# The first four feed-forward quanta of a fused attention and feed-forward kernel, laid side by side in four PSUM banks around AV of the fourth head pair

## The chip, the core and the metric

The kernel runs on one core of a Trainium2 chip. The metric is the device time of one execution in microseconds (us), as the median of several runs. One further execution was recorded by the hardware profiler; all durations and waits below come from it. The engines are named as in the profile: PE is TensorE (matmuls; PEld its weight loads), DVE is VectorE, ACT is ScalarE, POOL is GpSimd and SP is SyncE, which here only issues DMAs.

## What is computed

Attention with a relative-position bias, and then a bilinear feed-forward layer on its output:

```python
B, H, S, D = 8, 8, 576, 64
scores = (1 / sqrt(D)) * matmul(q, k.transpose(0, 1, 3, 2))
scores = scores + bias_table[bucket].transpose(2, 0, 1)[None]
attn = exp(scores - max(scores)); attn = attn / (sum(attn) + 1e-09)
attn_out = matmul(attn, v)
x = attn_out.transpose(0, 2, 1, 3).reshape(B * S, H * D)      # 4608 x 512
return (x @ w_a) * (x @ w_b) @ w_out                           # 512 -> 1536 -> 512
```

## The kernel before

The work of attention is cut into 32 head pairs (batch b, pair hp of heads 2hp and 2hp+1), numbered p = 4b + hp. For each pair: q and k are brought into the layout "channels on partitions" (`emit_transposes_first` and `emit_transposes` on PE for p below 10, a transposing DMA after that), scores are computed transposed (`emit_scores`, four tiles st_0 to st_3 of 128 keys by 2 x 512 queries; `emit_scores_rest`, st_4 and st_5 for what is left over), ACT takes their exponential into a tile `at`, DVE multiplies in the exponential of the bias where it isn't constant (`emit_mult`), and PE multiplies with v (`emit_av`, ten groups per pair, called AV here). A column of ones beside v gives the sums; DVE divides by them (L331, L333) into a tile `xg`. `emit_x` transposes `xg` into `xn`, the transposed x that the feed-forward needs: on PE with a copy by DVE for the first batch, by a transposing DMA for the others. Head pair hp of a batch gives the 128 rows `xn[:, hp, ...]`, so the sum over the 512 model channels has four parts, mc = 0 to 3, and part mc needs only head pair mc.

The feed-forward works on nine chunks c of 512 tokens. It is written as a generator, `ffn_quanta`, of 36 quanta a chunk, each of four matmuls of 512 columns: for each of 12 blocks df of the hidden channels a quantum "pa" (x times w_a, four parts mc, into one PSUM bank; ACT copies the bank to a tile `ha`) and a quantum "pb" (x times w_b; DVE multiplies the bank by `ha` into `g`), and then 12 quanta "po" (`g` times w_out, three quanta to one output tile, which DVE copies and SP sends out). Quanta are pulled one by one with `next(quanta)` and so fill PE between the steps of attention.

The order on each engine is written by hand (a manual schedule): every engine works through its instructions in the order of emission, and semaphores only delay them. PSUM has eight banks of 2 KB a partition. Four of them are a ring of two slots with two banks each (`pst`, tag "st"), for the scores and the transposes of q and k. The other four are single banks, m0 to m3, given out in turn by `bank(use, ...)`: at first m0 and m1 to the use "av" (AV results, transposes of x), m2 and m3 to "ffn".

The first four pairs (batch 0) run in the loop at L442. The feed-forward can't start before all four pairs have their rows in `xn`: L475 to L485 emit x of pair 2, AV of pair 3, x of pair 3, and only then the first two quanta (pa 0, pb 0), the transposes of pair 4's q and k, and two more quanta (pa 1, pb 1). From there "av" has the bank m0 alone and "ffn" has m1, m2 and m3. `QUANTA_FIRST` says how many quanta of the first chunk are done by then (4). The main loop at L498 has nine places s for each pair from p = 4 on; at each place it emits scores (s = 0, 3, 6), multiplications (s = 2, 5, 8), perhaps a quantum (L522: the remaining 36 - QUANTA_FIRST quanta of the first chunk are spread over the first 47 places, from then on each place has one), and parts of AV of the pair before (`AV_AT`, `AV_LAST`). In pair 5 at s = 3, `relayout_qk(1, 4, 8)` (L525) lets DVE copy q and k of pairs 6 and 7 into the layout that their transposes (`emit_transposes`, L219) read; it stands behind the quantum of its place. The loads of v, of q and k and of the weights are issued by POOL in a fixed order; later loads are held back by `pace(p)`, a small copy on POOL that waits for the last multiplication of a pair.

Of the kernel before, what the change touches and what calls it, by code (L numbers as in the profile page):

```python
# [13 lines left out]
def kernel(  # L14
# [11 lines left out]
    nc = tc.nc  # L26
    FP32 = mybir.dt.float32
    BF16 = mybir.dt.bfloat16
    ACTF = mybir.ActivationFunctionType
    MULT = mybir.AluOpType.mult  # L30
# [3 lines left out]
    B, H, S, Dh = 8, 8, 576, 64  # L34
# [4 lines left out]
    NDF = DF // 128  # L39
    NMC = DM // 128  # L40
# [8 lines left out]
    wrk = ctx.enter_context(tc.tile_pool(name="wrk", bufs=2))  # L49
    pst = ctx.enter_context(tc.tile_pool(name="pst", bufs=2, space=PSUM))  # L50
# [5 lines left out]
    def bank(use, shape, dtype, name):  # L56
        turn[use] += 1
        return pone.tile(shape, dtype, tag=f"m{banks[use][turn[use] % len(banks[use])]}", name=name)
# [79 lines left out]
    wa_sb = wpool.tile([128, NMC, DF], BF16, name="wa")  # L138
    wb_sb = wpool.tile([128, NMC, DF], BF16, name="wb")
# [63 lines left out]
    xn = wpool.tile([128, NMC, NT + 64], BF16, name="xn")  # L203
# [21 lines left out]
    def emit_transposes_first(p, k_act=False, ring=False):  # L225

        b, hp = pairs[p]
        qkT = wrk.tile([128, 2, S], BF16, tag="qkT", bufs=3, name=f"qkT{p}")
        qkT_of[p], qT_of[p], kT_of[p] = qkT, qkT[:, 0, :], qkT[:, 1, :]
        both = pst.tile([128, 2, 1024], BF16, tag="st", name=f"tr{p}") if ring else None  # L230
        for which, t in enumerate(qk_tiles[b][0:2]):
            if ring:
                ps = both[:, which, :]
            else:
                ps = bank("ffn", [128, 1024], BF16, f"tr{p}_{which}")
            for j in range(LJ):
                for hh in range(2):
                    nc.tensor.transpose(ps[64 * hh:64 * hh + 64, LP * j:LP * j + LP],
                                        t[:, 2 * hp + hh, Dh * j:Dh * j + Dh], ident[0:LP, 0:LP])
            o = qkT[:, which, :].rearrange("c (p j) -> c p j", j=LJ)  # L240
            i = ps[:, 0:S].rearrange("c (j p) -> c p j", j=LJ)
            if ring:
                if which:
                    nc.scalar.activation(
                        out=qkT[:, :, :].rearrange("c w (p j) -> c w p j", j=LJ),
                        in_=both[:, :, 0:S].rearrange("c w (j p) -> c w p j", j=LJ), func=ACTF.Copy)
            elif which == 0 or k_act:
                nc.scalar.activation(out=o, in_=i, func=ACTF.Copy)
            else:
                nc.vector.tensor_copy(out=o, in_=i)  # L250

    def emit_tails(p):

        for hh in range(2):
            r = slice(64 * hh, 64 * hh + 64)
            nc.vector.tensor_copy(out=bd2[p % 2][r, :, r], in_=qkT_of[p][r, :, 512:S])
# [51 lines left out]
    def emit_av(p, gidx):  # L308

        b, hp = pairs[p]  # L310
        at, vb = at2[p % 2], vb2[b % 2]
        jq, hh = gidx // 2, gidx % 2
        if gidx in (0, 6):
            n = 3 if gidx == 0 else 2
            av_state[p] = bank("av", [128, n, 2, Dh + 1], FP32, f"av{p}_{gidx}")
        pav = av_state[p]
        j = jq if jq < 3 else jq - 3
        if hh == 0:

            nc.tensor.matmul(out=pav[:, j, :, :], lhsT=at[:, 8, 128 * jq:128 * jq + 128],  # L320
                             rhs=vb[:, 2 * hp:2 * hp + 2, 4, :], start=True, stop=False)
        for i in range(4):
            nc.tensor.matmul(out=pav[:, j, hh, :], lhsT=at[:, 2 * i + hh, 128 * jq:128 * jq + 128],  # L323
                             rhs=vb[:, 2 * hp + hh, i, :], start=False, stop=(i == 3 and hh == 1))
        if gidx in (5, 9):
            n = 3 if gidx == 5 else 2
            j0 = 0 if gidx == 5 else 3
            if gidx == 5:
                xg_of[p] = wrk.tile([128, 5, 128], BF16, tag="xg", name=f"xg{p}")
            rc = wrk.tile([128, 3, 2, 1], FP32, tag="rc", name=f"rc{p}_{gidx}")  # L330
            nc.vector.reciprocal(out=rc[:, 0:n, :, :], in_=pav[:, :, :, Dh:Dh + 1])  # L331
            xo = xg_of[p][:, j0:j0 + n, :]
            nc.vector.tensor_tensor(out=xo.rearrange("p j (h d) -> p j h d", h=2),  # L333
                                    in0=pav[:, :, :, 0:Dh],
                                    in1=rc[:, 0:n, :, :].to_broadcast([128, n, 2, Dh]), op=MULT)

    def emit_x(p):

        b, hp = pairs[p]
        if b > 0:  # L340

            nc.sync.dma_start_transpose(
                out=xn[:, hp, S * b:S * b + 640].rearrange("p (j t) -> p j t", j=5),
                in_=xg_of[p][:, :, :].rearrange("p j t -> p (j t)"))
            return
        ps = bank("av", [128, 5, 128], BF16, f"xT{p}")
        for jq in range(5):
            nc.tensor.transpose(ps[:, jq, :], xg_of[p][:, jq, :], ident[:, :])
        nc.vector.tensor_copy(out=xn[:, hp, S * b:S * b + S],  # L349
                              in_=ps[:, :, :].rearrange("p j t -> p (j t)")[:, 0:S])  # L350


    def ffn_bank(name):
        return bank("ffn", [128, 512], FP32, name)

    def ffn_quanta(c):
        g = wrk.tile([128, NDF, 512], BF16, tag="g", name=f"g{c}")
        for df in range(NDF):
            ps = ffn_bank(f"pa{c}_{df}")
            for mc in range(NMC):  # L360
                nc.tensor.matmul(out=ps[:, :], lhsT=wa_sb[:, mc, 128 * df:128 * df + 128],  # L361
                                 rhs=xn[:, mc, 512 * c:512 * c + 512],
                                 start=(mc == 0), stop=(mc == NMC - 1))
            ha = wrk.tile([128, 512], FP32, tag="ha", name=f"ha{c}_{df}")
            nc.scalar.activation(out=ha[:, :], in_=ps[:, :], func=ACTF.Copy)  # L365
            yield
            ps = ffn_bank(f"pb{c}_{df}")
            for mc in range(NMC):
                nc.tensor.matmul(out=ps[:, :], lhsT=wb_sb[:, mc, 128 * df:128 * df + 128],  # L369
                                 rhs=xn[:, mc, 512 * c:512 * c + 512],  # L370
                                 start=(mc == 0), stop=(mc == NMC - 1))
            nc.vector.tensor_tensor(out=g[:, df, :], in0=ps[:, :], in1=ha[:, :], op=MULT)  # L372
            yield
        for tt in range(4):
            ps = ffn_bank(f"po{c}_{tt}")
            for part in range(3):
                for df in range(4 * part, 4 * part + 4):
                    nc.tensor.matmul(out=ps[:, :], lhsT=g[:, df, 128 * tt:128 * tt + 128],  # L378
                                     rhs=wo_sb[:, df, :], start=(df == 0), stop=(df == NDF - 1))
                if part == 2:  # L380
                    ob = wrk.tile([128, DM], FP32, tag="ob", name=f"ob{c}_{tt}")
                    nc.vector.tensor_copy(out=ob[:, :], in_=ps[:, :])  # L382
                    r0 = 512 * c + 128 * tt
                    nc.sync.dma_start(out=out[r0:r0 + 128, :], in_=ob[:, :])
                yield

    def all_quanta():
        for c in range(NCH):
            yield from ffn_quanta(c)

    quanta = all_quanta()


    warm = const.tile([128, 512], BF16, name="warm")
# [8 lines left out]
            nc.tensor.matmul(out=wp[:, :], lhsT=warm[:, 0:128], rhs=warm[:, :], start=True, stop=True)  # L403


    QUANTA_FIRST = 4

    emit_warm(6)
    qk_alloc(0)
# [27 lines left out]
    def emit_avs(p, g0, g1):  # L437
        for g in range(g0, g1):
            emit_av(p, g)


    for p in range(4):  # L442
        emit_scores(p, 0)
        emit_scores(p, 1)
        if p:
            emit_mult(p, 0)
            emit_mult(p, 1)
            if p > 1:
                emit_x(p - 2)
                emit_avs(p - 1, 0, 4)  # L450
        else:
            emit_warm(3)
# [19 lines left out]
        emit_mult(p, 4)  # L472
        if p < 3:
            emit_tails(p + 1)
    emit_x(2)  # L475
    emit_avs(3, 0, 10)
    emit_x(3)
    banks.update(av=(0,), ffn=(2, 3, 1))
    next(quanta)
    next(quanta)  # L480
    emit_transposes_first(4, ring=True)
    emit_tails(4)
    relayout_qk(1, 2, 4)
    for _ in range(QUANTA_FIRST - 2):
        next(quanta)  # L485


# [10 lines left out]
    for p in range(4, NP + 1):  # L498
        if p < NP:
            b, hp = pairs[p]  # L500
# [5 lines left out]
        for s in range(9):  # L506
# [14 lines left out]
            n = 9 * (p - 4) + s  # L521
            if n >= 47 or (n + 1) * (36 - QUANTA_FIRST) // 47 > n * (36 - QUANTA_FIRST) // 47:  # L522
                next(quanta, None)
# [66 lines left out]
```

## Time and profile before

| | |
|---|---|
| time, median of 3 runs | 419.52 us (418.82 to 420.39) |
| the profiled execution's own time | 419.12 us |
| its span, first to last instruction | 417.4 us |
| PE busy | 402.5 us, 96% of the span |
| DVE busy | 233.9 us, 56% |
| ACT busy | 231.2 us, 55% |
| POOL busy | 79.0 us, 19% |
| granted PE clock, mean | 0.998 |

How to read the lines that follow: a line of a timeline has the start in us from the span's start, the length in us, the engine, the line in the kernel, the operation, what it writes and reads, shape and type, the number of instructions merged into it, and in brackets the idle time of the engine just before with what ended it. The end of a matmul is modelled, and matmuls overlap: one of 512 columns is shown with 379 ns, but the next starts 216 ns after it. A few matmul records are missing from the trace, so that a group of four can show three. A line of the stretches has a start and an end in us, the length, the busy time of each engine, the granted clock and the work of the DMA engines.

### The profile page before, as it was taken

How to read it: one execution, taken by the hardware profiler on the slowest of the kernel's cores; microseconds unless marked ns; L12 is line 12 of the kernel's file. 1: busy time of each engine (PE TensorE's matmuls, PEld its weight loads, DVE VectorE, ACT ScalarE, POOL GpSimd, SP SyncE). 2: the span in 40 equal slices, each digit the busy share in tenths (PEclk: the TensorE clock that was granted, in tenths of full speed). 3: DMA queues.
4: the chain of work that ended last, by engine and by line, in shares of the span. 5: the costliest groups of instructions: out<-in, count | busy, mean ns of one | idle time of the engine just before them, and what ended most of it. 6: DMA issues, size and time to landing. Idle time of an engine off the chain costs nothing.

```text
span 417.4 us, 8452 instructions
## 1 busy us (share of the span) xinstructions
PE 402.5 (96%) x3346; PEld 206.4 (49%) x3404; DVE 233.9 (56%) x568; ACT 231.2 (55%) x313; POOL 79.0 (19%) x136
## 2 busy tenths in 40 slices
PE   8789899999999999999999999999999999999996
PEld 2455355555455455454555555454554554444442
DVE  3486666676555755575556656665556553332331
ACT  4984788566755665476646674567556631321320
POOL 8744641113111311103011311130000000000000
PEclk9999999999999999999999999999999999999999
DMA  9999999699759686978697977983342012002002
GB/s 111 183 209 206 166 189 105 135 208 158 107 94 207 114 100 104 213 102 112 102 178 136 134 103 151 177 127 52 71 121 45 17 40 93 2 0 101 2 0 101
DMA packets 111176, 47.71 MB, mean 114 GB/s; under 512 B 85120, under 2 KB 106528, under 8 KB 111136
## 3 DMA queue, kind: packets, MB, share of 16 engines
q0 software_dynamic: 54304, 18.88, 42.2%
q1 hardware_dynamic: 56832, 28.29, 28.0%
q8 instruction: 26, 0.43, 0.4%
q14 instruction: 14, 0.11, 0.1%
HBM read 38.77 MB, written 16.19 MB: 132 GB/s over the span
## 4 chain that ended last, share of the span: by engine, by line
PE 85%; DMA 8%; POOL 3%; issue 2%; DVE 1%; ACT 1%; POOLq 0%; DVEq 0%
PE po L378 23%; PE pb L369 21%; PE pa L361 21%; PE av L323 8%; PE st L267 7%; DMA wb<-in_moe_w_b_dram 6%; PE av L320 2%; DMA vb<-in_v_dram 2%; PE st L285 2%; PE st L277 1%; POOL vb L129 1%; POOL kl L108 0%; PE tr L219 0%; POOL ql L108 0%; ACT at L269 0%
## 5 line engine op out<-in xcount | busy, mean ns | idle before, releaser
L269 ACT ACTIVATE at<-st 128x1024 bf16<-128x1024 f32 x128 | 124.0, 1022 | 52.1 <-PE st L267 51.2
L372 DVE TENSOR_TENSOR g<-pb,ha 128x512 bf16<-128x512 f32 x108 | 74.6, 691 | 77.0 <-PE pb L369 54.0
L365 ACT ACTIVATE ha<-pa 128x512 f32<-128x512 f32 x108 | 64.7, 599 | 92.2 <-PE pa L361 91.0
L369 PE MATMUL pb<-xn,wb 128*128 128x512 bf16 x407 | 109.0, 379 | 1.5
L361 PE MATMUL pa<-xn,wa 128*128 128x512 bf16 x417 | 108.8, 379 | 0.5
L378 PE MATMUL po<-wo,g 128*128 128x512 bf16 x415 | 99.7, 379 | 0.8
L303 DVE TENSOR_TENSOR at<-at,E 128x768 bf16<-128x768 bf16 (+2 forms) x128 | 61.5, 501 | 7.9 <-DMA E<-tab_scratch 4.1
L323 PE MATMUL av<-vb,at 128*128 128x65 bf16 x1280 | 64.7, 194 | 0.3 <-DVE at L303 0.2
L378 PEld LDWEIGHTS <-g 128*128 128x128 bf16 x432 | 39.6, 98 | 49.1 <-issue 7.9
L323 PEld LDWEIGHTS <-at 128*128 128x128 bf16 x1280 | 55.4, 98 | 16.5 <-issue 1.2
L369 PEld LDWEIGHTS <-wb 128*128 128x128 bf16 x432 | 38.7, 97 | 46.4 <-issue 8.0
L361 PEld LDWEIGHTS <-wa 128*128 128x128 bf16 x432 | 38.4, 97 | 43.2 <-issue 7.0
L382 DVE COPY ob<-po 128x512 f32<-128x512 f32 x36 | 24.9, 691 | 53.9 <-PE po L378 53.9
L267 PE MATMUL st<-qkT 64*128 64x512 bf16 x256 | 40.8, 385 | 2.6 <-ACT at L280 0.9
L320 PE MATMUL av<-vb,at 128*128 128x130 bf16 x160 | 35.4, 221 | 2.5 <-DVE xn L349 1.2
L496 POOL COPY pace<-at 1x1 bf16<-1x1 bf16 x22 | 4.2, 193 | 173.0 <-DVE at L303 172.9
L333 DVE TENSOR_TENSOR xg<-av,rc 128x384 bf16<-128x384 f32 x64 | 31.4, 491 | 2.2
L129 POOL DMA_DIRECT2D vb<-in_v_dram x36 | 30.7, 864 | 7.9 <-PE pb L369 2.2
L280 ACT ACTIVATE at<-st 128x512 bf16<-128x512 f32 x32 | 19.1, 597 | 23.0 <-PE st L277 23.0
L331 DVE RECIPROCAL rc<-av 128x6 f32<-128x6 f32 x64 | 11.8, 184 | 27.6 <-PE av L323 27.6
L320 PEld LDWEIGHTS <-at 128*128 128x128 bf16 x160 | 15.6, 98 | 17.1 <-issue 1.6
L287 ACT ACTIVATE at<-st 128x576 bf16<-128x576 f32 x32 | 20.7, 646 | 0.0
(51 smaller groups left out, 177.8 us busy)
## 6 DMA issues: line engine op xcount, KB each, us to landing
out_dram<-ob SPq DMA_DIRECT2D x36, 256.0 KB, 2.3
qk_scratch<-qkn SPq DMA_DIRECT2D x22, 288.0 KB, 4.5
ql<-in_q_dram POOLq DMA_DIRECT2D x15, 288.0 KB, 5.7
kl<-in_k_dram POOLq DMA_DIRECT2D x15, 288.0 KB, 6.9
vb<-in_v_dram POOLq DMA_DIRECT2D x28, 128.0 KB, 6.7
wa<-in_moe_w_a_dram POOLq DMA_DIRECT2D x4, 384.0 KB, 13.9
wb<-in_moe_w_b_dram POOLq DMA_DIRECT2D x4, 384.0 KB, 13.6
wo<-in_moe_w_out_dram POOLq DMA_DIRECT2D x4, 384.0 KB, 7.9
```

Source lines behind the costliest of these rows:

```text
L129: nc.gpsimd.dma_start(out=vb2[b % 2][:, h0:h1, i, 0:Dh], in_=v[b, h0:h1, 128 * i:128 * i + 128, :].transpose([1, 0, 2]))
L267: nc.tensor.matmul(out=st[:, hh, :], lhsT=kT[r, 128 * i:128 * i + 128], rhs=qT[r, 0:512], start=True, stop=True)
L269: nc.scalar.activation(out=at[:, 2 * i:2 * i + 2, 0:512], in_=st[:, :, :], func=ACTF.Exp, scale=scale)
L303: nc.vector.tensor_tensor(out=at[:, sl, q0:q0 + w], in0=at[:, sl, q0:q0 + w], in1=e, op=MULT)
L320: nc.tensor.matmul(out=pav[:, j, :, :], lhsT=at[:, 8, 128 * jq:128 * jq + 128], rhs=vb[:, 2 * hp:2 * hp + 2, 4, :], start=True, stop=False)
L323: nc.tensor.matmul(out=pav[:, j, hh, :], lhsT=at[:, 2 * i + hh, 128 * jq:128 * jq + 128], rhs=vb[:, 2 * hp + hh, i, :], start=False, stop= ...
L333: nc.vector.tensor_tensor(out=xo.rearrange("p j (h d) -> p j h d", h=2), in0=pav[:, :, :, 0:Dh], in1=rc[:, 0:n, :, :].to_broadcast([128, n ...
L361: nc.tensor.matmul(out=ps[:, :], lhsT=wa_sb[:, mc, 128 * df:128 * df + 128], rhs=xn[:, mc, 512 * c:512 * c + 512], start=(mc == 0), stop=( ...
L365: nc.scalar.activation(out=ha[:, :], in_=ps[:, :], func=ACTF.Copy)
L369: nc.tensor.matmul(out=ps[:, :], lhsT=wb_sb[:, mc, 128 * df:128 * df + 128], rhs=xn[:, mc, 512 * c:512 * c + 512], start=(mc == 0), stop=( ...
L372: nc.vector.tensor_tensor(out=g[:, df, :], in0=ps[:, :], in1=ha[:, :], op=MULT)
L378: nc.tensor.matmul(out=ps[:, :], lhsT=g[:, df, 128 * tt:128 * tt + 128], rhs=wo_sb[:, df, :], start=(df == 0), stop=(df == NDF - 1))
```

## The change

The first four quanta of the first chunk (pa 0, pb 0, pa 1, pb 1) are no longer emitted one after the other when all of x is there. They are opened together, in four PSUM banks (both banks of one slot of the score ring, and m2 and m3), and each head pair's part mc of the four sums is emitted as soon as that pair's rows of x are there: part 0 after x of pair 2 and ahead of AV of pair 3, part 1 after that AV, parts 2 and 3 after x of pair 3. The copies and products that empty the four banks follow part 3. The transposes of pair 4's q and k come after these four quanta instead of after two, and two more quanta (pa 2, pb 2) follow them, so that six are done before the main loop; the spread over its first 47 places has 30 quanta instead of 32, and the places where a quantum stands move. The copy that puts pair 2's rows into `xn` goes from DVE to ACT.

```diff
-    def emit_x(p):
+    def emit_x(p, act=False):
...
-        nc.vector.tensor_copy(out=xn[:, hp, S * b:S * b + S],
-                              in_=ps[:, :, :].rearrange("p j t -> p (j t)")[:, 0:S])
+        o, i = xn[:, hp, S * b:S * b + S], ps[:, :, :].rearrange("p j t -> p (j t)")[:, 0:S]
+        if act:
+            nc.scalar.activation(out=o, in_=i, func=ACTF.Copy)
+        else:
+            nc.vector.tensor_copy(out=o, in_=i)
...
-    def ffn_quanta(c):
-        g = wrk.tile([128, NDF, 512], BF16, tag="g", name=f"g{c}")
-        for df in range(NDF):
+    class EarlyQuanta:
+
+
+        def __init__(self):
+            self.g = wrk.tile([128, NDF, 512], BF16, tag="g", name="g0")
+            ring = pst.tile([128, 2, 512], FP32, tag="st", name="pab0_0")
+            self.ps = [(ring[:, 0, :], ring[:, 1, :]),
+                       tuple(ffn_bank(f"{n}0_1")[:, :] for n in ("pa", "pb"))]
+
+        def part(self, mc):
+            for df in range(2):
+                for ps, w_sb in zip(self.ps[df], (wa_sb, wb_sb)):
+                    nc.tensor.matmul(out=ps, lhsT=w_sb[:, mc, 128 * df:128 * df + 128],
+                                     rhs=xn[:, mc, 0:512], start=(mc == 0), stop=(mc == NMC - 1))
+                if mc == NMC - 1:
+                    ha = wrk.tile([128, 512], FP32, tag="ha", name=f"ha0_{df}")
+                    nc.scalar.activation(out=ha[:, :], in_=self.ps[df][0], func=ACTF.Copy)
+                    nc.vector.tensor_tensor(out=self.g[:, df, :], in0=self.ps[df][1], in1=ha[:, :],
+                                            op=MULT)
+
+    def ffn_quanta(c, early=None):
+        g = early.g if early else wrk.tile([128, NDF, 512], BF16, tag="g", name=f"g{c}")
+        for df in range(2 if early else 0, NDF):
...
-    def all_quanta():
+    def all_quanta(early):
         for c in range(NCH):
-            yield from ffn_quanta(c)
-
-    quanta = all_quanta()
+            yield from ffn_quanta(c, early if c == 0 else None)
...
-    QUANTA_FIRST = 4
+    QUANTA_FIRST = 6
...
-    emit_x(2)
+    emit_x(2, act=True)
+    early = EarlyQuanta()
+    early.part(0)
     emit_avs(3, 0, 10)
+    early.part(1)
     emit_x(3)
+    early.part(2)
+    early.part(3)
+    quanta = all_quanta(early)
     banks.update(av=(0,), ffn=(2, 3, 1))
-    next(quanta)
-    next(quanta)
     emit_transposes_first(4, ring=True)
     emit_tails(4)
     relayout_qk(1, 2, 4)
-    for _ in range(QUANTA_FIRST - 2):
+    for _ in range(QUANTA_FIRST - 4):
         next(quanta)
```

In the changed kernel the matmuls of the four early quanta are L371, their copies L375 and products L376; the copy of x on ACT is L351; the later quanta are L384 (pa), L388 (ha), L392 (pb), L395 (g) and L401 (po).

## The prediction

> **What bounds the kernel now.** I read the busy shares first, then the stretches of time, then the timeline of each engine where the change works.
>
> ```profile
> PE 402.5 (96%) x3346; PEld 206.4 (49%) x3404; DVE 233.9 (56%) x568; ACT 231.2 (55%) x313; POOL 79.0 (19%) x136
> ```
>
> That is each engine's busy time. Next, by stretch: its length, then busy time of PE, of weight loads, of DVE, ACT and POOL, then the granted clock.
>
> ```profile
> 32.00:50.00 18.00, 16.06 (x154) 8.05 (x156) 11.02 (x27) 11.89 (x17) 9.01 (x13) 1.00 1.47 182
> 50.00:60.00 10.00, 9.76 (x113) 5.67 (x113) 7.21 (x18) 7.49 (x11) 6.13 (x10) 1.00 1.27 201
> 60.00:70.00 10.00, 9.89 (x102) 5.47 (x101) 7.28 (x19) 8.37 (x13) 2.39 (x5) 1.00 1.66 107
> ```
>
> TensorE (PE) is the bound. In the stretch that the change touches, 32 to 50 us, it is busy 16.06 of 18.00 us; from 50 us on it has almost no holes (9.76 and 9.89 of 10). So about 1.9 us of holes is what there is to fill, and 0.24 us in the ten after that. The granted clock is 1.00 in all three. The holes, from the timeline of PE:
>
> ```profile
> 32.19 0.23 PE L320 MATMUL av<-vb,at 128*128 128x130 bf16 x1 [0.49 <-ACT at L287]
> ...
> 34.18 0.34 PE L348 MATMUL xT<-ident,xg 128*128 128x128 bf16 x3 [0.17 <-DVE xg L333]
> 34.75 0.28 PE L348 MATMUL xT<-ident,xg 128*128 128x128 bf16 x2 [0.23 <-DVE xg L333]
> ...
> 43.16 0.39 PE L267 MATMUL st<-qkT 64*128 64x512 bf16 x2 [0.57 <-ACT qkT L221]
> ...
> 49.75 0.22 PE L320 MATMUL av<-vb,at 128*128 128x130 bf16 x1 [0.67 <-DMA vb<-in_v_dram]
> ```
>
> The first is AV of the fourth pair waiting for the last exponential of its scores, the next two are the transposes of x waiting for VectorE (DVE). The fourth is a chain on ScalarE (ACT), the fifth a transfer of v that landed at 49.62 us. The last two lie behind the change; whether they give back what it gains is the question.
>
> **The change part by part.** A quantum is four 512-column matmuls; from 37.39 (pa) to 38.26 (pb) it takes 0.87 us, 0.216 a matmul. I count when PE reaches a place and how many quanta it has done by then; a quantum done early is worth 0.865 us.
>
> Step 1, the gain. Before, PE is free at about 31.6 us (end of the transposes of pair 2) and starts its second "pa" at 37.39, having done AV (five groups of two at 0.32: 1.6 us), five transposes (0.35), two quanta (1.73) and 24 transposes of q and k (0.73): 4.41 us of work in 5.79, so 1.38 us of holes. After, four quanta stand in the same stretch: 3.46 + 1.6 + 0.35 + 0.73 = 6.14 us. The first four matmuls wait only for the exponential L280, which ended at 31.59, and run until 32.5, past the end of L287 (32.14): the 0.49 is gone. The second four run while DVE divides (its last xg ends near 35.0), the third while it copies the last rows of x (near 36.0). Weights: those of rows 2 and 3 are asked for at 35.3 as before. PE is through at about 37.78, 0.39 later with 1.73 us more done: 1.34 us ahead.
>
> The copy of pair 2's x goes to ACT. No row has it; the nearest are the copy of the same shape in L248 (0.66 on ACT) and the DVE copy that it replaces (0.45). I take 0.66: it lies in a 3.86 us hole of ACT (32.14 to 36.00) and ends near 32.7, before the AV group that needs its bank (33.46). Free; without that hole it would cost up to 0.66, against 0.45 saved on DVE. The Trainium skill, "ScalarE: Activation LUTs", Rules for kernel authors, gives plain element work to VectorE, which speaks against this edit; the rows agree that ACT is the dearer (0.66 against 0.45), and an estimate by that rule would be 0.2 us worse, but the hole of 3.86 us decides.
>
> The two score banks that the first "pa" and "pb" borrow were emptied at 31.59 and are read out by 38.0; scores of pair 4 ask for them at 39.6: no wait. The two "ha" copies, 0.49 apart, end at 37.7, before the copy of q and k (L244) can start. "pb" 2 wants the bank of the second product at 38.65, when that is just read (36.95 + 0.38 for the last matmul, two DVE products of 0.69 behind the copies): no wait, or under 0.1. SP and POOL keep their order; only the pacing copies on POOL come up to a microsecond later, and the v that they pace is used some 30 us on.
>
> Step 2, the ACT chain takes one quantum back.
>
> ```profile
> 39.65 1.94 ACT L269 ACTIVATE at<-st 128x1024 bf16<-128x1024 f32 x2 [0.54 <-PE st L267]
> 41.48 0.60 ACT L365 ACTIVATE ha<-pa 128x512 f32<-128x512 f32 x1
> 41.95 1.15 ACT L221 ACTIVATE qkT<-tr 128x1152 bf16<-128x1152 bf16 x1
> 42.96 1.98 ACT L269 ACTIVATE at<-st 128x1024 bf16<-128x1024 f32 x2
> ```
>
> From the first scores of pair 4 (39.22) to its fourth score tile (43.16, which needs the bank that L221 empties) ACT works without a hole: 3.94 us, whatever PE does. Before, PE has two quanta and a transpose in that stretch; in the changed order only one quantum ("pa" 3), since the spread of 30 instead of 32 quanta over 47 places moves "pb" 3 behind the fourth tile. So PE reaches it at 43.55 with 7 quanta instead of 43.16 with 6: ahead 0.865 - 0.39 = 0.48.
>
> Step 3, it is given again at the v transfer. AV of pair 4 stood at 49.75, of which 0.78 us was idle. Now "pb" 5 and "pa" 6 come before it instead of "pa" 5, and it starts at 50.14, past the landing at 49.62, with 13 quanta done instead of 11: ahead 1.34.
>
> Step 4, a new wait on DVE.
>
> ```profile
> 51.20 0.69 DVE L372 TENSOR_TENSOR g<-pb,ha 128x512 bf16<-128x512 f32 x1 [0.73 <-remote]
> 51.80 0.71 DVE L116 COPY qkn<-ql 96x768 bf16<-96x768 bf16 x2
> 52.44 0.98 DVE L116 COPY qkn<-kl 96x768 bf16<-96x768 bf16 x2
> ```
>
> Those four copies of q and k feed the transposes of pair 6 on PE (53.05 before, no wait). In the changed order of DVE they stand behind the product of "pb" 6, and on PE "pb" 6 is followed only by one AV group and then those transposes. "pb" 6 ends issue at 52.26; its product runs 52.45 to 53.14, the first copy ends at 53.41, so the transposes, ready at 52.67, wait 0.8 us; their second half needs the third copy (54.05 to 54.2) and waits 0.35 to 0.5 more. Behind them on PE queues everything; behind the copies on DVE queues xg of pair 4, which costs the next AV group 0 to 0.2. From 50.14: four quanta 3.46, the rest 3.41, waits 1.2 to 1.4: PE starts pair 6 at 58.2 to 58.4 with 17 quanta, before at 57.64 with 16. Ahead 0.1 to 0.3.
>
> Step 5, a second one like it. In pair 6 "pb" 9 now directly precedes AV's third group, and DVE has its product ahead of the division of that group. "pb" 9 ends issue at 63.3; its product runs 63.5 to 64.2, the division ends at 64.3, xg at 64.9; the single AV bank is wanted at 64.5: a wait of 0.43. Transposes of pair 7 wait 0.13 for a score bank, about as the fourth score tile did before (0.1). Pair 7 then starts 1.03 to 1.23 later with one quantum more: 0.17 to 0.37 behind. In pair 7 two holes of before (0.18 for the AV bank, 0.12 for a score bank) shrink to one of 0.12, and by pair 8 both orders have done 28 quanta: 76.3 to 76.5 against 76.28. From there to the end the order is the same but for neighbours.
>
> Sum: 0.1 us slower, so nothing. The profiled execution took 419.12 us (span 417.4), 0.4 under the median 419.52; against it the sum gives 419.2, and against the median 419.6, which I forecast. What a measurement of this kernel can tell from no change is about 0.5%, 2.1 us.
>
> **The rivals.** The gain is kept: steps 4 and 5 do not bite, because DVE has the copies done when PE wants them. For it: DVE is busy only 7.2 of 10 us there. Against it: its order is fixed and the product needs "pb" 6. Then 1.2 to 1.4 and 0.43 us come off: 1.5 faster, 418.0.
>
> DVE's copies are slow: all four at 0.49, as the pair at 52.44 while POOL issues. The third copy then ends near 54.5, AV of the second half waits for xg, and pair 5 and pair 6 lose 0.4 to 0.8 more: 420.2.
>
> The interleaved matmuls do not keep the pitch. Before, four in a row fill one bank; L371 changes bank and weights each time, and AV cuts the sums in two. Lower end: 0.216 us, since the weight load (0.098) hides behind a matmul as in L361, and AV changes weights each time too. Upper end: the full 0.379 that one takes. 16 x 0.163 = 2.6 us: 422.2, slower; it decides by itself from a pitch of about 0.34 us. I take 0.216, because in every row of 512 columns the bank's last matmul is followed at that pitch by the next bank's first. The Trainium skill, "TensorE: Matmul & The Clock Gate", A second HAM failure mode, says that cycling through banks can leave short idle moments which make the clock fall to half; by that rule one window of 3.4 us at half rate would cost, as an estimate from that page, 1.7 us. The granted clock of 1.00 beside holes of 0.78 us speaks against it.
>
> **How the numbers follow.** No change as summed (419.0 to 420.0): 0.70. Gain kept, wholly or in part (417.8 to 419.0): 0.14. Slow copies (420.0 to 420.6): 0.10. Lost pitch: 0.04; the rest 0.02. The range runs from 418.3, most of the kept gain, to 420.6. Faster by over 0.5% needs 2.1 us, more than all the holes of 32 to 50 us: 0.03. Slower by over 0.5% is lost pitch and the unforeseen: 0.05. Within: 0.92.
>
> **What would show it.** Right: no idle before AV of the fourth pair; a longer wait for L221 at its fourth score tile of pair 4 (about 1.2 us for 0.57); no wait for v; a new wait of PE for L116 of about 0.8 us near 52.7, and one for xg near 64.5; 28 quanta done near 76.4. Wrong: the wait for L116 missing (then faster), or starts of L371 more than 0.22 us apart (then slower).

## The result, and the profile after

The changed kernel takes 421.9 us (median of 22 runs, 420.04 to 424.69), the kernel before 419.35 in the same session (22 runs, 418.24 to 422.86): a ratio of 1.0047, 95% interval 1.003 to 1.0064. So it is slower by about 2.0 us (1.3 to 2.7), not equal, and above the 420.6 at which the forecast range ended. (The two medians alone lie 2.55 us apart; the ratio with its interval, taken over the runs, is what I go by.) The profiled execution took 422.53 us, with a span of 420.8.

First the busy times, and then the same three stretches, moved by 1.68 us, since the fourth pair's last score tile (st_5 of pair 3, the last point ahead of the change) starts 1.68 us later in this profile, at 32.48 us for 30.81. The columns are as before. Ahead of the three stand two rows of the front, 10 to 32 us, of the kernel before and of the changed one.

```profile
PE 405.5 (96%) x3404; PEld 207.8 (49%) x3404; DVE 231.5 (55%) x567; ACT 231.6 (55%) x314; POOL 79.0 (19%) x136
```

```profile
10.00:32.00 22.00, 17.65 (x280) 11.38 (x281) 15.08 (x44) 20.23 (x27) 13.25 (x24) 1.00 1.30 195
...
10.00:32.00 22.00, 16.87 (x257) 11.75 (x256) 13.79 (x40) 17.56 (x24) 13.63 (x23) 0.84 1.30 192
33.70:51.70 18.00, 16.64 (x155) 8.45 (x154) 9.38 (x25) 12.26 (x18) 9.39 (x14) 1.00 1.50 193
51.70:61.70 10.00, 8.99 (x98) 4.94 (x97) 6.18 (x19) 7.29 (x11) 2.46 (x5) 1.00 1.47 192
61.70:71.70 10.00, 9.53 (x104) 5.13 (x102) 6.72 (x19) 7.91 (x11) 3.08 (x6) 1.00 0.80 67
```

The stretch of the change is fuller, as it was meant to be (PE busy 16.64 of 18.00 us for 16.06). The next two have holes that were not there: 1.0 and 0.5 us for 0.24 and 0.11. The first two rows are a stretch of the front, whose code both kernels share: its granted clock is 1.00 before and 0.84 here. The 0.84 comes from a half clock from 14.9 to 21.7 us, which the profile of before does not have; the control below shows that the change has no part in it.

The waits of PE behind the change, from its timeline:

```profile
43.73 0.39 PE L267 MATMUL st<-qkT 64*128 64x512 bf16 x2 [0.24 <-ACT at L269]
45.24 0.39 PE L267 MATMUL st<-qkT 64*128 64x512 bf16 x2 [1.12 <-ACT qkT L221]
55.28 0.97 PE L219 MATMUL tr<-ident,qkn 96*128 96x96 bf16 x12 [0.81 <-DVE qkn L116]
66.74 0.23 PE L320 MATMUL av<-vb,at 128*128 128x130 bf16 x1 [0.38 <-DVE xg L333]
...
91.17 0.38 PE L384 MATMUL pa<-xn,wa 128*128 128x512 bf16 x1 [0.56 <-DMA xn<-xg]
...
354.79 1.02 PE L384 MATMUL pa<-xn,wa 128*128 128x512 bf16 x4 [0.78 <-DVE ob L405]
```

The second, third and fourth are those that the prediction names, in the sizes that it gives; the first is a short wait for ACT ahead of the second. The last two it does not have. The fifth is the first "pa" of chunk 1, whose fourth part needs x of pair 7. The sixth stands far behind the change, at the first quantum of chunk 7, where attention is over and the feed-forward gets all four single banks. Before, the same place had no wait:

```profile
346.11 5.34 PE L378 MATMUL po<-wo,g 128*128 128x512 bf16 x23
351.29 1.03 PE L361 MATMUL pa<-xn,wa 128*128 128x512 bf16 x4
```

In both kernels 24 matmuls of "po" precede that "pa" (one record is missing here). 24 at 0.216 us are 5.18: before, "pa" follows at once (351.29); after, it comes 6.12 us behind the start of its "po" matmuls (348.67 to 354.79), 0.94 late.

The reason can be counted in the code. `bank` moves a turn on by one with each bank given out and takes the bank at that place of the list. The changed kernel takes two of the four early sums from the score ring, so two turns of "ffn" fewer are counted. When L582 of the kernel after (`banks["ffn"] = (0, 1, 2, 3)`) makes three banks into four, the count then stands so that the first "pa" of chunk 7 is given m3, the bank that the last "po" of chunk 6 has just filled, and which DVE copies out first (L405, 0.69 us). In the kernel before it was given m1, whose output tile DVE had copied out one tile, 2.6 us, sooner.

### The profile page after: what moved, and what is told of

The parts are those of the page before. It is cut to its first block, busy times and chain, and to the rows that moved or that the text cites. A ratio compares the mean times of both kernels' runs of the same rounds, so it can differ in the third digit from the quotient of the medians.

```text
span 420.8 us, 8508 instructions
## 1 busy us (share of the span) xinstructions
PE 405.5 (96%) x3404; PEld 207.8 (49%) x3404; DVE 231.5 (55%) x567; ACT 231.6 (55%) x314; POOL 79.0 (19%) x136
## 4 chain that ended last, share of the span: by engine, by line
PE 88%; DMA 5%; DVE 2%; ACT 2%; SPq 2%; issue 1%; DVEq 0%; ACTq 0%
PE pb L392 22%; PE po L401 22%; PE pa L384 22%; PE av L323 9%; PE st L267 7%; DMA E<-tab_scratch 2%; PE av L320 2%; PE st L285 2%; PE st L277 1%; SPq L188 1%; DMA xn<-xg 1%; ACT at L269 1%; DMA tab_scratch<-tab_sb 1%; DMA oh_sb<-oh_const 1%; PE tr L219 1%
## 5 line engine op out<-in xcount | busy, mean ns | idle before, releaser
L395 DVE TENSOR_TENSOR g<-pb,ha 128x512 bf16<-128x512 f32 x106 | 73.3, 691 | 83.9 <-PE pb L392 61.2
L388 ACT ACTIVATE ha<-pa 128x512 f32<-128x512 f32 x106 | 63.4, 598 | 93.0 <-PE pa L384 93.0
L384 PE MATMUL pa<-xn,wa 128*128 128x512 bf16 x424 | 109.0, 379 | 1.3 <-DVE ob L405 0.8
L392 PE MATMUL pb<-xn,wb 128*128 128x512 bf16 x424 | 109.0, 379 | 0.0
L401 PE MATMUL po<-wo,g 128*128 128x512 bf16 x432 | 101.2, 379 | 0.0
L323 PEld LDWEIGHTS <-at 128*128 128x128 bf16 x1280 | 56.3, 99 | 17.9 <-DVE at L303 2.6
L401 PEld LDWEIGHTS <-g 128*128 128x128 bf16 x432 | 39.7, 98 | 49.3 <-issue 7.4
L392 PEld LDWEIGHTS <-wb 128*128 128x128 bf16 x424 | 37.8, 97 | 47.2 <-issue 10.2
L384 PEld LDWEIGHTS <-wa 128*128 128x128 bf16 x424 | 38.0, 97 | 43.1 <-issue 6.6
L405 DVE COPY ob<-po 128x512 f32<-128x512 f32 x36 | 24.9, 692 | 53.4 <-PE po L401 53.4
L320 PEld LDWEIGHTS <-at 128*128 128x128 bf16 x160 | 15.7, 98 | 16.4 <-issue 2.2
```

## The experiments

Each kernel was run beside the kernel before, in five rounds. The fronts of the profiles differ by up to 3.4 us (st_5 of pair 3 starts between 30.81 and 34.20 us), so I compare distances: from the start of st_5 of one pair to that of a later pair, from PE's timeline. By pair 8 all orders have done the same 32 quanta. At pair 4 they have not: the orders with six quanta ahead of the main loop (after, e1, e3, e4, c4, x1) have done nine there, the others eight, and a quantum is 0.865 us; the first two columns are compared between orders with the same count, or added up.

| run | pair 3 to 4 | 4 to 8 | 8 to 9 | 31 to last matmul | ratio to before, 95% interval |
|---|---|---|---|---|---|
| before | 14.63 | 37.87 | 9.90 | 76.22 | 1 |
| c1, before again | 14.63 | 37.03 | 11.10 | 76.22 | 0.9993 [0.9974, 1.0013] |
| after | 15.04 | 37.62 | 10.63 | 77.09 | 1.0047 [1.003, 1.0064] |
| e1, turn back | 15.04 | 37.62 | 9.91 | 76.14 | 1.0025 [1.0003, 1.0048] |
| e2, turn alone | 14.45 | 37.04 | 11.09 | 77.09 | 1.0023 [0.9995, 1.0051] |
| e3, e1 and relayout first | 15.03 | 36.40 | 9.90 | 76.15 | 0.9998 [0.9975, 1.002] |
| e4, spread alone | 16.17 | 37.62 | 9.90 | 76.23 | 1.0059 [1.0032, 1.0085] |
| c2, four banks alone | 14.36 | 37.39 | 9.91 | 76.15 | 0.9978 [0.9953, 1.0003] |
| c3, earlier transposes | 13.83 | 38.32 | 11.57 | 76.15 | 1.0002 [0.998, 1.0025] |
| c4, e3 and AV first | 14.72 | 35.85 | 10.58 | 76.15 | 0.996 [0.9942, 0.9978] |
| x1, c4 and x of pair 7 | 15.04 | 35.84 | 9.91 | 76.14 | 0.9968 [0.9943, 0.9993] |
| x2, before and x of pair 7 | 14.64 | 37.33 | 9.91 | 76.22 | 0.9978 [0.9959, 0.9997] |
| x3, c3, relayout, x of pair 7 | 13.84 | 38.29 | 9.91 | 76.15 | 0.9995 [0.9973, 1.0018] |

In e2, e4 and c4 the half clock ended close ahead of st_5 of pair 3 (30.8 to 32.4 us), and this tile itself waited 0.2 to 0.3 us for ACT, as in no other run. That makes their first distance 0.2 to 0.3 short: 14.45 in e2 for 14.63 in the same order, 14.72 in c4 for 15.03.

From pair 9 to pair 31 the distance is 243.87 or 243.88 in all of them: nothing of the change is felt there.

### e1 and e2: the turn of the banks

e1 is the changed kernel with two turns skipped, e2 the kernel before with one turn skipped, which moves it into the bad place:

```diff
+    turn["ffn"] += 2        (e1; += 1 in e2)
     banks["ffn"] = (0, 1, 2, 3)
```

> The changed kernel with the count that hands out the feed-forward banks put on by two at the switch from three to four banks (the change had made two hand-outs fewer). Theory: the change loses about 2 us by three waits of its own, of which the first pa of chunk 7 waiting for the copy of the last po of chunk 6, in the same bank, is 0.9 us (seen as 0.78 idle). Then this run is 0.8 to 1.0 us (0.2%) faster than the changed kernel, 1.0 to 1.3 us (0.3%) slower than before, and no wait stands ahead of that pa. Rival, that the 2 us come from the half clock at the start: this run equals the changed kernel, 0.47% slower than before.

> The kernel before with the same count put on by one at the switch, so that the first pa of chunk 7 gets the bank of the last po of chunk 6. Theory: 0.8 to 1.0 us (0.2%) slower than before, with an idle of about 0.8 us ahead of that pa. Rival (the bank of the hand-out costs nothing, for the queue ahead covers it): equal to before.

The stretch from pair 31 to the last matmul says it without noise: 77.09 us falls to 76.14 in e1, and 76.22 rises to 77.09 in e2. In the profile of e1 the wait ahead of that "pa" is gone (first line); in e2 it stands in the kernel before, with the same releaser, the copy of the output tile (second line):

```profile
352.39 1.03 PE L384 MATMUL pa<-xn,wa 128*128 128x512 bf16 x4
...
354.66 1.02 PE L361 MATMUL pa<-xn,wa 128*128 128x512 bf16 x4 [0.78 <-DVE ob L382]
```

So the turn costs 0.87 us of PE and nothing else in the change is needed for it. In the times it is 0.2%: 1.0047 falls to 1.0025, and 1.0023 for the turn alone. The intervals overlap, and that of e2 reaches below 1; what separates the runs is the profiles.

### c1: the kernel before once more

> The kernel before, unchanged, run as a control. Theory: it equals the kernel before (ratio within 0.003 of 1), and its profile, as those of the other runs, has a stretch of half granted clock in the front; st_5 of pair 3 then starts at 31.5 to 33 us instead of 30.81, the wait of PE for the v transfer ahead of AV of the fourth pair (0.78 us in the profile of before) is shorter or gone, and pair 5 starts up to 1.0 us earlier relative to pair 3 than there. Rival: the early front of the profile of before is usual for the kernel before, and the later fronts of the changed kernels come from the change; then this profile has its pair 3 at 30.8 and the same 0.78 us wait.

```profile
10.00:32.00 22.00, 18.46 (x265) 12.42 (x260) 15.29 (x44) 18.45 (x26) 13.86 (x25) 0.84 1.30 194
```

```profile
49.14 0.22 PE L320 MATMUL av<-vb,at 128*128 128x130 bf16 x1
...
89.19 0.38 PE L361 MATMUL pa<-xn,wa 128*128 128x512 bf16 x1 [1.03 <-DMA xn<-xg]
```

These are the unchanged kernel's clock in front and two lines of PE's timeline. The half clock is there too (15.0 to 21.8 us), so the change does not bring it. AV of pair 4 starts at 49.14 without a wait; in the profile of before it started at 49.75, and behind st_5 of pair 4 it came 0.83 us later than here (4.31 for 3.48). The reason is in POOL's queue: the last part of that v was issued at 40.78 us here and at 42.42 there (L135), and landed at 48.17 and 49.62, while PE stood within 0.3 us of the same place. And at the first "pa" of chunk 1 the unchanged kernel waits 1.03 us for x of pair 7, longer than the changed kernel did.

One point of the expectation failed: pair 3 started at 31.03, not at 31.5 to 33, so the wait for v does not go with a late front of PE but with the lead of POOL. Two further profiles have the order of before up to there. In e2, v lands at 48.24 us, long before AV of pair 4 starts (50.99). In x2 it lands at 49.40 and AV follows at 49.54, 0.3 us later behind st_5 of pair 4 than in the control (3.78 for 3.48). So the wait on which the prediction set part of its sum was there in full in one of four executions, by a third in one, and not at all in two.

### e4 and c2: the two halves of the change

e4 is the kernel before with `QUANTA_FIRST = 6`: two more quanta ahead of the main loop and a spread of 30, but one after the other, as before. c2 has the four banks, the turn put back and `QUANTA_FIRST = 4`: nothing more ahead of the loop and the spread of before.

```diff
-    QUANTA_FIRST = 4        (e4, on the kernel before)
+    QUANTA_FIRST = 6
...
-    QUANTA_FIRST = 6        (c2, on the changed kernel)
+    QUANTA_FIRST = 4
...
+    turn["ffn"] += 2        (c2)
     banks["ffn"] = (0, 1, 2, 3)
```

> The kernel before with six quanta ahead of the main loop instead of four, all one after the other as before, and the remaining 30 spread over 47 places. Theory: it has the waits of the spread (copies of q and k in pair 5, product ahead of the division in pair 6, x of pair 7) without the 1.3 us that the early quanta gain: 1.3 to 2.2 us (0.3 to 0.5%) slower than before, and no wait at the switch of banks. Rival, that the side by side matmuls themselves cost: equal to before within 0.3 us.

> The changed kernel with the bank turn put back (two hand-outs skipped at the switch) and with two quanta fewer ahead of the loop: the four early quanta stand, none follows them, and the rest is spread as before the change. Theory: the early quanta come 1.3 us sooner to their end, but PE then waits some 1.3 us ahead of st_0 of pair 4 for ACT's copy of the transposed q and k (L244), so pair 4 starts no earlier than before and the time is within 0.2% of the kernel before. Rival (the matmuls around four banks lose pitch, or the product ahead of pair 4 delays it): 0.5 to 1 us slower than before. Rival (the wait for L244 isn't what ends last): 1.3 us faster, ratio 0.997.

e4 has the waits of the changed kernel behind pair 4, to the hundredth:

```profile
48.09 0.39 PE L267 MATMUL st<-qkT 64*128 64x512 bf16 x2 [1.12 <-ACT qkT L221]
58.12 0.97 PE L219 MATMUL tr<-ident,qkn 96*128 96x96 bf16 x12 [0.81 <-DVE qkn L116]
69.58 0.23 PE L320 MATMUL av<-vb,at 128*128 128x130 bf16 x1 [0.38 <-DVE xg L333]
```

and the same 37.62 us from pair 4 to pair 8. So those waits are the spread's, and the four banks have no part in them. With that spread, the four banks are worth 1.13 us up to pair 4 (15.04 for 16.17) and keep them to the end. That distance of e4 is one of the three that are short; with the 0.18 us by which e2 is short the gain is about 1.3. In the times, e1 against e4, run on one chip, is 1.0025 against 1.0059, with intervals that overlap.

Without the two quanta the gain has no place to go. PE reaches pair 4 early and waits for ACT's copy of its q and k, from the timeline of c2:

```profile
39.40 0.61 PE L267 MATMUL st<-qkT 64*128 64x512 bf16 x4 [1.23 <-ACT qkT L244]
43.33 0.39 PE L267 MATMUL st<-qkT 64*128 64x512 bf16 x2 [0.57 <-ACT qkT L221]
49.46 0.22 PE L320 MATMUL av<-vb,at 128*128 128x130 bf16 x1 [0.20 <-DMA vb<-in_v_dram]
```

0.27 us is left by pair 4. By pair 8 (from pair 3: 51.75) it stands within 0.1 us of the control (51.66). The ratio, 0.9978 with an interval that holds both 1 and the rival's 0.997, cannot choose; the wait of 1.23 us in the profile does, for the theory.

### e3 and c4: the order of DVE in pairs 5 and 6

e3 is e1 with the relayout of q and k ahead of the quantum of its place, so that the copies do not stand behind the product of "pb" 6. c4 is e3 with the AV groups of place 3 of pair 6 ahead of the quantum of that place, so that the division does not stand behind the product of "pb" 9.

```diff
+            if p == 5 and s == 3:
+                relayout_qk(1, 4, 8)                            (e3, c4)
+            if p == 6 and s == 3:
+                emit_avs(p - 1, *av_at.get(s, (0, 0)))          (c4)
             if n >= 47 or (n + 1) * (36 - QUANTA_FIRST) // 47 > n * (36 - QUANTA_FIRST) // 47:
                 next(quanta, None)
-            if p == 5 and s == 3:
-                relayout_qk(1, 4, 8)
...
             if p > 4:
-                emit_avs(p - 1, *av_at.get(s, (0, 0)))
+                if (p, s) != (6, 3):                            (c4)
+                    emit_avs(p - 1, *av_at.get(s, (0, 0)))
```

> As the first run, and in pair 5 the four copies of q and k are emitted ahead of the quantum of their place instead of behind it, so that on VectorE they do not stand behind the product of pb 6. Theory: the 0.81 us wait for the copies and the shorter wait for the third copy go, 1.1 to 1.3 us; unless the later wait for x of pair 7 takes it back, 0.0 to 0.2 us faster than before; if it does, 0.3 to 0.8 slower than before. Rival, that TensorE then waits elsewhere in pair 5 (ScalarE's copy L221): at most 0.4 us gained on the first run.

> The changed kernel with the bank turn put back, the relayout of pairs 4 to 8 of q and k ahead of the quantum in pair 5, and in pair 6 the AV group ahead of the quantum, so that the division of the AV doesn't stand behind the product. Theory: the three waits of the changed kernel in pairs 5 to 7 and at the last chunk are gone; 0.3 to 0.5 us faster than the run with the first two alone, ratio to before 0.998 to 1.0. Rival (the order of AV and quantum doesn't matter, since AV then waits for its own operands): equal to that run within 0.1 us in the starts of pair 7.

DVE after the change, at the place of the first of these waits, and DVE in e3:

```profile
54.27 0.69 DVE L395 TENSOR_TENSOR g<-pb,ha 128x512 bf16<-128x512 f32 x1 [1.50 <-PE pb L392]
54.88 0.61 DVE L116 COPY qkn<-ql 96x768 bf16<-96x768 bf16 x2
55.41 0.62 DVE L116 COPY qkn<-kl 96x768 bf16<-96x768 bf16 x2
```

```profile
52.54 1.06 DVE L116 COPY qkn<-ql 96x768 bf16<-96x768 bf16 x2
53.53 0.61 DVE L116 COPY qkn<-kl 96x768 bf16<-96x768 bf16 x2
54.12 0.69 DVE L395 TENSOR_TENSOR g<-pb,ha 128x512 bf16<-128x512 f32 x1
```

In the first, DVE idles 1.50 us for the "pb" while four copies that need nothing from it stand behind. In the second the copies come first. From pair 4 to pair 8 this is worth 1.22 us (37.62 to 36.40), and the times say 1.1 (1.0025 to 0.9998, on one chip, with intervals that overlap). The AV order gives 0.55 more (35.85). With c4 the changed kernel is faster than the kernel before: 418.66 us against 420.11, ratio 0.996 [0.9942, 0.9978]. That is better than the 0.998 to 1.0 expected. By the profiles, the control takes 51.66 us from pair 3 to pair 8, c4 50.57, and x1, which is the same up to there and has no short first distance, 50.88: 0.8 us ahead of the control, and 1.0 ahead of the mean of the four executions with the order of before (51.9). That is the lower end of what the interval gives (0.9 to 2.4 us).

### x1 and x2: x of pair 7

The first "pa" of chunk 1 waited for x of pair 7 in five of the ten profiles taken up to then (after, e2, c1, c3, c4: the distance from pair 8 to 9 is 0.7 to 1.7 us over 9.90), in both kernels, and not in the other five. The DMA is issued between 83.2 and 88.6 us and lands 4.0 to 6.3 us later; where it took 4.7 or less PE did not wait, where it took 5.3 or more it did. x1 (on c4) and x2 (on the kernel before) do AV of pair 7 a place sooner, and so issue that DMA sooner:

```diff
         av_at = AV_LAST if last else AV_AT
+        if p == 8:
+            av_at = {1: (0, 4), 2: (4, 6), 3: (6, 10)}
...
-                if s == (4 if last else 6):
+                if s == (3 if p == 8 else 4 if last else 6):
```

> The run c4 (bank turn put back, relayout and AV ahead of the quantum) with the AV groups of pair 7 in the steps 1, 2 and 3 of pair 8 in place of 1, 2 and 4, and its x behind them, so that the transposing DMA of x of pair 7 is issued one step, some 1.7 us, sooner. Theory: its landing, 4.6 to 6.3 us after the issue at 83.2 to 85.8 us in the profiles so far, is what the first pa of chunk 1 waited 0.7 to 1.5 us for in five of the ten; issued sooner it lands ahead of that matmul in the profile (no wait there), and the time is 0.2 to 0.7 us under that of c4, ratio to before 0.994 to 0.996. Rival: the landing is set by what else the queues carry then, not by the issue, or the wait moves to AV of pair 7; then the wait stays and the ratio is that of c4, 0.996 to 0.998.

> The kernel before with this one edit alone. Theory: the wait for x of pair 7 belongs to both kernels and comes by chance of the front and of the queues (0 in the profile of before, 1.0 us in that of its control), so the edit helps the kernel before as well: 0.2 to 0.8 us faster, ratio 0.998 to 0.9995, and no wait at the first pa of chunk 1 in its profile. Rival: the wait is the change's own, since it sets the quanta of chunk 1 earlier against x; then the kernel before gains nothing, ratio 1.0.

The landings took 5.1 and 5.4 us and PE waited in neither (9.91). The issue came 0.21 us ahead of st_5 of pair 8 in both, where it came 0.65 behind it in c4 and 0.52 in the control: sooner by 0.7 to 0.9 us, not by the 1.7 of the expectation, and enough. The kernel before gains, 0.9978 [0.9959, 0.9997], so this wait is its own and not the change's. x1 is not measurably faster than c4 (0.9968 and 0.996): half of the profiled executions had no such wait to lose, and c4's profiled one had 0.52 us of it.

### c3 and x3: a try at keeping the whole gain

c3 has the four banks, one quantum more ahead of the loop, and the transposes of pair 4 behind part 1 instead of part 3, so that ACT's copy L244 runs beside the parts. x3 is c3 with the relayout in place 1 of pair 5 and x of pair 7 issued sooner.

```diff
-    QUANTA_FIRST = 6
+    QUANTA_FIRST = 5
...
     early.part(1)
+    emit_transposes_first(4, ring=True)
     emit_x(3)
     early.part(2)
     early.part(3)
...
-    emit_transposes_first(4, ring=True)
...
+            if p == 5 and s == 1:                   (x3)
+                relayout_qk(1, 4, 8)
...
-            if p == 5 and s == 3:
-                relayout_qk(1, 4, 8)
...
+    turn["ffn"] += 2
     banks["ffn"] = (0, 1, 2, 3)
```

> The changed kernel with the bank turn put back, one quantum fewer ahead of the loop, and the transposes of pair 4 moved to right behind the second of the three parts of the early quanta, so that ACT's copy L244 runs beside the parts. Theory: with that wait hidden, the gain of the early quanta (1.3 us) is kept by pair 4 and no later wait of DVE in pairs 5 and 6 arises; 1.0 to 1.5 us faster than the kernel before, ratio 0.9965 to 0.998. Rival (the landing of the v transfer gates AV of pair 4 whatever PE does ahead of it): the gain is turned into a wait there, ratio 0.999 to 1.001.

> The run c3 (bank turn put back, transposes of pair 4 ahead of the third part of the early quanta, one quantum ahead of the loop) with its two later waits taken away: the relayout of pairs 4 to 8 goes to step 1 of pair 5, where DVE stood idle 1.16 us, and x of pair 7 is issued a step sooner. Theory: pair 4 starts 0.8 us earlier than in the kernel before relative to pair 3, and without the 0.70 us wait of AV of pair 5 for the division and the 1.5 us wait for x, that is kept to the end: 1.3 to 2 us faster than before, ratio 0.995 to 0.997. Rival (the landing of the v transfer sets AV of pair 4 here): the 0.8 us are gone by pair 5 whatever DVE does, ratio 0.998 to 1.0.

My theory fell in both. Pair 4 does start 0.80 us sooner (13.83 for 14.63), with no wait for L244, but from pair 4 to pair 8 both lose 1.3 us to the control (38.32 and 38.29 for 37.03). The rival, the landing of v, is not it either: neither profile lists a wait for v at AV of pair 4. The waits there are others in each, and with 1.23 and 1.22 us in all they are nearly the whole loss (c3 first, then x3):

```profile
54.05 0.23 PE L320 MATMUL av<-vb,at 128*128 128x130 bf16 x1 [0.70 <-DVE xg L333]
61.14 0.39 PE L267 MATMUL st<-qkT 64*128 64x512 bf16 x2 [0.27 <-ACT qkT L221]
70.79 0.39 PE L267 MATMUL st<-qkT 64*128 64x512 bf16 x2 [0.26 <-ACT qkT L221]
```

```profile
56.76 0.41 PE L285 MATMUL st<-qkT,bd 128*128 128x288 bf16 x2 [0.68 <-ACT qkT L221]
63.30 0.39 PE L267 MATMUL st<-qkT 64*128 64x512 bf16 x2 [0.27 <-ACT qkT L221]
72.95 0.39 PE L267 MATMUL st<-qkT 64*128 64x512 bf16 x2 [0.27 <-ACT qkT L221]
```

In x3, moving the relayout removed the wait for the division and put one of the same size for ACT's copy of the transposes in its place. A spread of 31 quanta sets each quantum against other steps of attention than 32 or 30 do; that this is what brings the new waits is my reading, not tried.

## Why the prediction was wrong

**Step 1 was right.** The first round of L371, its end, and what follows each, from PE's timeline of the kernel after:

```profile
33.32 0.38 PE L371 MATMUL pab<-xn,wa 128*128 128x512 bf16 x1
33.54 0.38 PE L371 MATMUL pab<-xn,wb 128*128 128x512 bf16 x1
33.75 0.38 PE L371 MATMUL pa<-xn,wa 128*128 128x512 bf16 x1
33.97 0.38 PE L371 MATMUL pb<-xn,wb 128*128 128x512 bf16 x1
34.18 0.22 PE L320 MATMUL av<-vb,at 128*128 128x130 bf16 x1
...
38.40 0.38 PE L371 MATMUL pb<-xn,wb 128*128 128x512 bf16 x1
38.70 0.45 PE L238 MATMUL tr<-ident,ql 96*64 96x96 bf16 x12
```

The pitch is 0.21 to 0.22 us across four banks, and AV follows at that pitch: the rival of lost pitch is out. 24 transposes end near 39.34, where "pa" 2 starts; less the 1.68 us of the front that is 37.66, for 37.78 predicted. The wait of 0.49 for the last exponential is gone, and so are those of the transposes of x. The gain against the same order without the four banks is 1.13 us as measured (e4), and about 1.3 with the first distance of e4 put right, for 1.34.

**The clock.** The granted clock in the stretch of the four banks is 1.00. The rule that the prediction weighed against the rows (the Trainium skill, "TensorE: Matmul & The Clock Gate", A second HAM failure mode: a kernel that cycles through PSUM banks idles for short moments between its groups, often enough that the clock swings between half and full) does not show here; the half clock of the front stands in the unchanged kernel as well.

**Steps 2, 4 and 5 were right in place and size.** The fourth score tile of pair 4 waits 1.12 us for L221, for about 1.2 predicted, and starts 12.76 us after st_5 of pair 3, for 43.55 - 30.81 = 12.74. The transposes of pair 6 wait 0.81 for L116, for 0.8, and their second half some 0.3 more, for 0.35 to 0.5 (the next "pa" starts 0.80 behind the first of them, where transposes of a pair without a wait take 0.51). AV in pair 6 waits 0.38 for the division, for 0.43. The cause named for them, DVE's order behind the products of "pb" 6 and "pb" 9, is shown by e3 and c4: with that order changed, the waits go. The first scores of pair 8 start at 78.07 us, less the 1.68 of the front 76.39, for 76.3 to 76.5: against the profile of before, the sum of the five steps came out.

**Step 3 was right for the one execution and wrong as a basis.** It says that the 0.78 us ahead of AV of pair 4 go, and they are gone. But they were idle time of the kernel before in the profiled execution; of three others with the same order, two had none of it and one 0.3 us. The prediction then set the sum made against that execution, "0.1 us slower", on the median as well ("against the median 419.6"). From pair 3 to pair 8 the changed kernel takes 52.66 us in both its executions (after, e1). That is 0.16 behind the profile of before, but 1.00 behind the control, 1.17 behind e2 (whose first distance is 0.18 short) and 0.69 behind x2: 0.8 on average. That the sum agreed with the one profile it was made from was in part the luck of that execution.

**The step that failed outright is the last sentence of step 5: "From there to the end the order is the same but for neighbours."** The order is the same, but the banks are not: two turns fewer were counted, and at the switch from three banks to four PE waits for a bank, 0.87 us (e1, e2). The prediction looked for waits where instructions had moved. It never followed the count that hands the banks out, although the change takes two sums out of that count in plain sight. With the turn put back the ratio is 1.0025 (e1), which on the median of before is 420.4 us (419.5 to 421.4), inside the forecast range.

Together: 0.8 us by pair 8 (1.0 against the control) and 0.87 us at the switch are 1.6 to 1.9 us, and the times give 2.0 (1.3 to 2.7). The wait for x of pair 7 comes and goes in both kernels and adds nothing on average that these runs could show.

**The rivals.** The gain was not kept. Slow copies on DVE (0.4 to 0.8 us more) did not come: the copies took 0.61 and 0.62 a pair. The copy of pair 2's x on ACT took 0.66 us, ending at 34.36, before AV needed its bank (35.12): free, as priced.

The forecast of no change had a chance of 0.92 since every loss was looked for inside 32 to 80 us. The slower side, 0.05, held lost pitch and the unforeseen; a bank hand-out disturbed by the change is a mechanism that could have been named and priced there, by one copy of DVE (0.69 us) and the way to it.

## What to carry to other kernels

Where buffers are given out in turn by a counter, a change that takes one hand-out more or fewer shifts every later hand-out; follow the counter to each place where the list changes its length, however far behind the change. Work done early is worth only what the next waits leave of it: here the four banks save 1.1 to 1.3 us, and the two quanta that use the saving cost that and more until the turn was put back and two orders on DVE were turned round (c4, 0.4% faster than before). And a wait in one profile is idle time of that execution: before a sum counts on its going, look whether a second execution of the same kernel has it.

## What the runs showed of the hardware

- The granted clock falls to half for 3.4 or 6.8 us somewhere in the first 33 us of nearly every profiled execution (at 15.0, 16.4, 18.0, 25.6, 27.6 us among others), and there not at all in two; the code of these 33 us is the same in all. The start of st_5 of pair 3 varies from 30.81 to 34.20 us. The Trainium skill, "TensorE: Matmul & The Clock Gate", Part 1, has a window of about 3.4 us that runs free of the kernel's start; the lengths here agree with one and two such windows.
- One transposing DMA of x (L342, the same bytes) landed 4.0 to 6.3 us after its issue at the same place of the program, in ten executions.
- The same v transfer was issued 1.6 us sooner or later in two executions of one kernel, POOL's queue against PE's, and landed 1.45 us sooner or later (48.17 and 49.62 us); that alone made or removed a wait of 0.8 us.
